# Scores of two heads through two shared buffers of two banks in a fused attention and soft-MoE kernel

## The chip, the cores and the metric

The kernel runs on one core of a Trainium2 chip. The time is device time in microseconds (us) of one execution of the whole program. A core has five engines that run their own queues of instructions: PE (matrix products; its weight loads are shown apart as PEld), DVE and ACT (element by element, with reductions on DVE), POOL (element by element too) and SP, which here only issues DMAs. On-chip memory is SBUF (128 partitions, 24 buffers of 8 KB a partition play a part here) and PSUM, where PE writes: eight banks of 128 x 512 float32.

## The reference

Attention with a local window and a few global keys, and its output, as 3072 tokens of 512, goes through a mixture of experts in which every slot is a softmax-weighted mean of all tokens:

```python
scores = scale * np.matmul(q, k.transpose(0, 1, 3, 2))            # B, H, S, D = 4, 8, 768, 64
rel = pos[:, None] - pos[None, :]
is_global = pos[None, :] < int(n_global)                          # 8 keys
is_local = (rel >= 0) & (rel < int(n_local))                      # 96 keys
scores = scores + -slopes[:, None, None] * dist                   # a slope for each head
scores = np.where(is_global | is_local, scores, -1000000000.0)
a = softmax(scores, axis=-1);  x = np.matmul(a, v)                # x: 3072 x 512
logits = x @ phi                                                  # 3072 x 32 slots
d = softmax(logits, axis=0);  c = softmax(logits, axis=1)
slot_in = d.T @ x                                                 # 8 experts x 4 slots, 512 wide
slot_out[e] = np.maximum(slot_in[e] @ w1[e], 0.0) @ w2[e]         # 512 -> 1024 -> 512
return c @ slot_out
```

(The softmaxes are abbreviated.) Everything is float32, and the products of attention weights and V are done to nearly that precision.

## The kernel before

**Units.** Attention is cut into 16 units, one for each batch b and pair of heads p. A unit's 768 queries are taken in seven blocks of keys (j); each block needs only the queries near it, so the scores of one head are seven matrices that stand side by side in 1296 columns, keys on the partitions.

**Steps of a unit u.** Each is a small function, and each issues one or a few instructions:

- `load_qk`, `load_v`: DMAs on SP's queue, into two alternating buffers for q and k and into the single buffer `vt` for V.
- `v_hi` (POOL, L490) and `v_lo` (DVE, L497): V times 64 as a float16 and the float16 of what is left of it.
- `scores(u)` (PE, L518): fourteen float32 products, seven for each head, each written as two matmuls in the profile. Head i has its own PSUM buffer `sc[i]` of three banks.
- `biased(u, i)` (DVE, L525): the eviction of head i. One custom instruction adds the table of biases and masks to 128 x 1296 scores, writes the sum to SBUF and leaves the greatest value of each partition in column i of `mx`. A small instruction behind it reads the accumulator.
- `max_t`, `max_r`, `max_b`, `max_c`: the two columns of maxima are transposed on PE (L533, into columns of `sc[1]` that the scores leave free), reduced to one number a head on DVE (L537), spread over two columns on DVE (L538), brought to all partitions on PE (L541) and copied to SBUF by ACT (L545). This maximum over a head of a unit is taken off in the exponential.
- `exponential(u, i)` (ACT, L548), `w_hi` (ACT, L551, the float16 of the weights), `w_lo` (POOL, L555, the float16 of what is left, in three parts a head; some parts are put on DVE as `w_lo_dve`).
- `values(u, i)` (PE, L575): 39 float16 matmuls, high by high, high by low and low by high, into one bank `x`. A column of ones in V gives the sums of the weights.
- `ev_sum`, `ev_rec`, `ev_mul` (DVE, L580, L584, L590): the sums, their reciprocals, and the eviction times the reciprocals into `xn`.
- `tr`, `tr_copy` (PE L603, ACT L608): x transposed in two halves, of four and three blocks; `logits` (PE L633, every second unit), and at the end of a batch the softmax pieces (`strip_...`, `by_token`) and the weighted sum of tokens (`dispatch`).

**What sets the order.** No scheduler does. The table `ORDER` (L51, 608 steps before) is a list of steps with their units, written by hand, and it is run from front to end:

```python
    for name, u, *args in ORDER:
        steps[name](u, *args)
```

So the order of the table is the order of the instructions on each engine, SP's DMAs included. The units overlap: around the maximum of unit u stand low parts and values of units u - 1 and u - 2. Engines wait for each other through semaphores where a buffer must be written or become free.

**Buffers.** Four float32 buffers `tp` hold the biased scores and later the weights of a head, and, in their last columns, the float16 high parts (two of them) and low parts (the other two). One bank holds `x`, one bank (`psm`) the transposes, logits and the rest, six the scores.

**The experts.** Their weights are 32 pieces of 1.05 MB. Twelve have buffers of their own (`wp`, `NW = 12`); twelve more places are attention's own buffers, which `free` steps load, part by part, when attention has used them for the last time. The parts of these buffers that attention doesn't use at all are loaded earlier, one at a time behind `load_v` (`extras`). Eight pieces are left. They take the places of pieces of the first layer once the first four experts' hidden layer has read them: four pieces in halves into places 0 to 3, four in quarters into places 4 and 8 to 10. Behind attention come the hidden layer (`hidden`, L106), its transposes (L120), the combining weights by slot (`weights_by_slot`, L170), the second layer (`project`, L136), its outputs (`slots_out`, L181) and the combination (`combine`, L196 to L202) with the output's DMAs.

## Time and profile before

| what | value |
|---|---|
| median of 3 runs | 238.98 us (236.74 to 241.77) |
| the profiled execution: span | 237.6 us (the page gives no other time of it) |
| PE, PEld busy | 185.2 us (78%), 142.3 us (60%) |
| DVE busy | 156.6 us (66%) |
| ACT, POOL busy | 120.4 us (51%), 118.8 us (50%) |
| DMA | 61.39 MB, 258 GB/s on the mean |
| instructions | 6476 |

A busy share is the time in which an engine ran something, as a share of the span. In the views that follow, a line such as `L525` is a line of the kernel's file, a group's row gives count, busy us, mean ns of one and the idle time just before its instructions with what ended it, and the chain of waits gives start, length, engine, buffer and line of each piece of the path that ended last. The page names a buffer without its number, so `sc` stands for both of them.

Over the whole span the profile divides into three: until about 31 us the first unit comes up, from there to about 174 us the units follow each other, some 10 us end attention and start the experts, and the last 53 us are the experts. POOL has work only until the end of attention.

### The profile page before, as it was taken

What the parts mean: (1) busy time and instruction counts of PE and PEld (TensorE: products, weight loads), DVE (VectorE), ACT (ScalarE), POOL (GpSimd) and SP (SyncE); (2) the same over time, 40 slices, a digit from 0 to 9 for tenths busy, and PEclk for the clock granted to TensorE, in tenths of its full rate; (3) what the DMA queues carried; (4) which work ended last, traced back from release to release, by engine and by line L of the source; (5) the groups of instructions that cost most, each with busy time, mean ns of one, the idle gap of its engine ahead of it and who ended that gap; (6) DMA issues with size and microseconds to landing.
All of it is one profiled execution on the core that took longest, in us unless ns stands there. A gap on an engine that the chain in (4) does not pass through costs nothing.

```text
span 237.6 us, 6476 instructions
## 1 busy us (share of the span) xinstructions
PE 185.2 (78%) x2676; PEld 142.3 (60%) x2676; DVE 156.6 (66%) x375; ACT 120.4 (51%) x167; POOL 118.8 (50%) x142
## 2 busy tenths in 40 slices
PE   8463869599698887988985987887688999999800
PEld 2453859587586776876864876766555326666600
DVE  4766192966859759669878696796757783524710
ACT  2001553758839557787764796778522155212500
POOL 7310067395959949978984888889300000000000
PEclk9965555999979999999999999997999999999975
DMA  5795784499996967257336168589799699938895
GB/s 159 274 405 196 316 321 179 125 394 349 372 390 194 415 259 242 69 203 251 103 129 217 21 229 290 151 261 304 254 302 393 206 392 400 384 111 278 293 338 169
DMA packets 20630, 61.39 MB, mean 258 GB/s; under 512 B 1904, under 2 KB 9200, under 8 KB 19056
## 3 DMA queue, kind: packets, MB, share of 16 engines
q1 hardware_dynamic: 20448, 60.89, 71.8%
q8 instruction: 23, 0.38, 0.6%
q14 instruction: 15, 0.12, 0.1%
q10 hardware_dynamic: 144, 0.00, 0.0%
HBM read 54.59 MB, written 6.29 MB: 256 GB/s over the span
## 4 chain that ended last, share of the span: by engine, by line
PE 45%; DVE 29%; issue 8%; POOL 7%; DMA 4%; ACT 2%; DVEq 0%; POOLq 0%; SPq 0%
PE sc L518 17%; DVE tp L525 13%; PE op L136 6%; PE hp L106 6%; PE x L575 6%; DVE v L497 5%; POOL tp L555 4%; DMA vt<-in_v_dram 3%; PE sc L533 2%; PE m L603 2%; DVE mr L537 2%; PE ctp L170 2%; DMA out_dram<-tp 1%; DVE rc L584 1%; DVE mm L538 1%
## 5 line engine op out<-in xcount | busy, mean ns | idle before, releaser
L555 POOL TENSOR_TENSOR tp<-tp 128x432 f16<-128x432 f32 x45 | 49.7, 1132 | 25.2 <-DVE tp L562 17.5
L555 POOL TENSOR_TENSOR tp<-tp,tp 128x432 f16<-128x432 f32 x44 | 49.0, 1140 | 12.7 <-ACT tp L551 8.4
L575 PEld LDWEIGHTS <-tp 128*128 128x128 f16 x1248 | 45.3, 102 | 13.7 <-DVE xmax L590 11.1
L575 PE MATMUL x<-v,tp 128*128 128x65 f16 (+1 forms) x1209 | 46.0, 199 | 8.9 <-DVE xmax L590 8.1
L518 PE MATMUL sc<-raw 64*128 64x216 f32 (+2 forms) x448 | 47.0, 365 | 1.6 <-DMA raw<-in_qk_dram 1.6
L518 PEld LDWEIGHTS sc<-raw 64*128 64x128 f32 x448 | 44.4, 212 | 5.2 <-DMA raw<-in_qk_dram 2.5
L548 ACT ACTIVATE tp<-tp,nb 128x1296 f32<-128x1296 f32 x32 | 44.1, 1377 | 0.6
L551 ACT CAST tp<-tp 128x1296 f16<-128x1296 f32 x30 | 38.2, 1274 | 7.0 <-PE x L575 6.2
L537 DVE TENSOR_REDUCE mr<-sc 2x1 f32<-2x128 f32 x16 | 4.5, 278 | 32.4 <-PE sc L518 32.4
L525 DVE CUSTOM_DVE_ANT_1 tp<-sc,tt 128x1296 f32<-128x1296 f32 x16 | 23.8, 1498 | 1.0 <-POOL tp L555 0.9
L603 PE MATMUL m<-ident,xn 120*128 120x120 f32 x109 | 17.8, 281 | 8.4 <-DVE xmax L590 6.1
L490 POOL TENSOR_SCALAR v<-vt 128x896 f16<-128x896 f32 x16 | 15.0, 940 | 14.5 <-DMA vt<-in_v_dram 12.2
L608 ACT COPY xta<-m 128x480 f32<-128x480 f32 (+1 forms) x21 | 10.1, 480 | 20.4 <-PE m L603 20.3
L590 DVE CUSTOM_DVE_ANT_1 xn<-x,rc 120x448 f32<-120x448 f32 x31 | 19.3, 623 | 1.0
L497 DVE SCALAR_TENSOR_TENSOR v<-vt,v 128x896 f16<-128x896 f32 x16 | 18.4, 1150 | 1.2 <-POOL v L490 1.2
L603 PEld LDWEIGHTS m<-ident,xn 120*128 120x128 f32 x109 | 11.3, 143 | 10.9 <-issue 4.9
L545 ACT COPY nb<-sc 128x2 f32<-128x2 f32 x16 | 2.6, 161 | 28.5 <-DVE mx L525 20.0
L533 PE MATMUL sc<-ident,mx 128*2 128x64 f32 x64 | 7.0, 239 | 8.6 <-DVE mx L525 8.1
L541 PE MATMUL sc<-mm,bsel 128*128 128x2 f32 x32 | 6.3, 266 | 8.2 <-DVE mm L538 7.3
L525 DVE CUSTOM_DVE_ANT_1 tp<-sc,xtt 128x1296 f32<-128x1296 f32 x8 | 12.0, 1499 | 0.5 <-POOL tp L555 0.4
L525 DVE CUSTOM_DVE_ANT_1 tp<-sc,vt 128x1296 f32<-128x1296 f32 x8 | 12.0, 1497 | 0.0
L541 PEld LDWEIGHTS sc<-mm,bsel 128*128 128x128 f32 x32 | 5.2, 203 | 11.2 <-DVE mm L538 8.4
(191 smaller groups left out, 263.6 us busy)
## 6 DMA issues: line engine op xcount, KB each, us to landing
raw<-in_qk_dram SPq DMA_DIRECT2D x15, 832.0 KB, 5.5
wp<-in_w_dram SPq DMA_DIRECT2D x12, 1024.0 KB, 9.5
vt<-in_v_dram SPq DMA_DIRECT2D x16, 448.0 KB, 4.1
wp<-in_w_dram SPq DMA_DIRECT2D x8, 512.0 KB, 8.3
wp<-in_w_dram SPq DMA_DIRECT2D x16, 256.0 KB, 5.4
out_dram<-tp SPq DMA_DIRECT2D x8, 512.0 KB, 6.7
tp<-in_w_dram SPq DMA_DIRECT2D x4, 648.0 KB, 5.5
out_dram<-vt SPq DMA_DIRECT2D x4, 512.0 KB, 4.2
```

The source lines that it names most:

```text
L106: nc.tensor.matmul(out=hp[n][32 * s:32 * s + 32, :], lhsT=slv(a, c, s), rhs=w1(e, c // 2)[:, (c % 2) * DF + 512 * n:(c % 2) * DF + 512 * n ...
L136: nc.tensor.matmul(out=o[32 * s:32 * s + 32, 0:w], lhsT=ht[:, c, 32 * s:32 * s + 32], rhs=w2(4 * a + s, half)[:, c0 + c * w:c0 + c * w + w ...
L490: nc.gpsimd.tensor_scalar(out=vhi[u % 2][:, :, :, 0:D], in0=vraw, scalar1=V_SC, scalar2=0.0, op0=ALU.mult, op1=ALU.add)
L497: nc.vector.scalar_tensor_tensor(out=vlo[k].rearrange("p j i d -> p (j i) d"), in0=vraw.rearrange("p j i d -> p (j i) d"), scalar=V_SC, in ...
L518: nc.tensor.matmul(out=sc[i][:, bk, at:at + n], lhsT=r_[r, KCOL[j]:KCOL[j] + KR], rhs=r_[r, KW + KB * j:KW + KB * j + n], start=True, stop ...
L525: nc.vector.tensor_tensor_reduce(out=tb(u, i).rearrange("p (k c) -> p k c", k=3), in0=sc[i][:, :, 0:BW], in1=table.banks(2 * (u % NP) + i) ...
L548: nc.scalar.activation(out=tb(u, i), in_=tb(u, i), func=AF.Exp, bias=nbs[u][:, i:i + 1], scale=T_SC)
L551: nc.scalar.copy(out=blocks(phi_[i])[:, :, 0:QW], in_=tb(u, i).rearrange("p (s c) -> p s c", c=QW))
L555: (engine or nc.gpsimd).tensor_tensor(out=blocks(plo_[i])[:, c, 0:QW], in0=tb(u, i).rearrange("p (s c) -> p s c", c=QW)[:, c], in1=blocks( ...
L575: nc.tensor.matmul(out=x[:, (D + 1) * t:(D + 1) * t + d], lhsT=w[:, c:c + P], rhs=vv[:, j, i, 0:d], start=(z == 0), stop=(z == len(ops) - ...
L590: nc.vector.tensor_tensor_reduce(out=xnb[(u // 2) % 3][:, :, c:c + D], in0=xps.pop((u, i))[:, :, 0:D], in1=rcs.pop((u, i)).unsqueeze(2).to ...
L603: nc.tensor.transpose(out=m[:, at:at + KB], in_=xnb[(u // 2) % 3][:, t, P * (p % 2):P * (p % 2) + P], identity=ident[0:KB, 0:KB])
```

## The change

- **Scores.** `scores(u, k)` makes a third of a unit's scores, for both heads: the blocks of bank k. The two buffers `sc[0]` and `sc[1]` have two banks each, one bank a head, and are used in turn over all thirds of all units.
- **Evictions.** `biased(u, k)` evicts a third for both heads at once, 128 x 2 x 432. The second and third take the running maximum of the one before as the start value, read from memory (`mx[:, k-1:k]`). The buffer that they write holds both heads; there are three such buffers `tb`, used in turn by units. The float16 parts are in two buffers of their own, `ph0` and `ph1`.
- **Maximum.** One maximum for both heads: one transposing matmul (L534) into a bank of `psm`, one reduction (L537) straight into the operand of the next matmul, one column broadcast. The instruction that spread two maxima (L538 of before) is gone, and so is the second matmul of each step. Both heads' exponentials use the same column.
- **Values.** `xx` has two banks, one a head. `ev_sums` and `ev_recs` take both heads in one instruction each. `psm` has two banks.
- **V.** `vt` holds two units' V, in halves, used in turn.
- **Weights.** `NW` is 9 and thirteen attention buffers become places, so 22 pieces of 32 have one before the hidden layer and ten take places over: five in halves into places 0 to 4, five in quarters into places 8 to 12. Parts unused by attention are loaded by `extra` steps of their own. `free` steps carry 11.90 MB of weights at the end of attention, where they carried 11.15.
- **Order.** The table is new, 629 steps. All six low parts of unit 0 are on POOL (three were on DVE), and in units 14 and 15 five parts are on DVE.

The core of the diff:

```diff
-NW = 12
+NW = 9
-ORDER = [('load_qk', 0), ('load_v', 0), ('load_qk0', 0), ('load_qk', 1), ('keys', 0), ('v_hi', 0), ('scores', 0),
+ORDER = [('load_qk0', 0), ('load_phis', 0), ('load_qk', 0), ('load_v', 0), ('keys', 0), ('load_qk', 1),
...
-    psm = banks.enter_context(tc.tile_pool(name="psm", bufs=1, space=PSUM))
+    psm = banks.enter_context(tc.tile_pool(name="psm", bufs=2, space=PSUM))
...
-    tps = [keep.tile([P, TW + PW // 2], F32, name=f"tp{i}") for i in range(4)]
+    tbt = [keep.tile([P, 2 * TW], F32, name=f"tb{i}") for i in range(3)]
+    pht = [keep.tile([P, WP], F32, name=f"ph{i}") for i in range(2)]
...
-    vraw = vt[:, 0:VC].rearrange(by_head, j=NJ, i=2)
+    vraw = [vt[:, VC * i:VC * i + VC].rearrange(by_head, j=NJ, i=2) for i in range(2)]
...
     def load_v(u):
-        nc.sync.dma_start(out=vraw, in_=v[u // NP, u % NP])
-        if u > 2 and extras:
+        nc.sync.dma_start(out=vraw[u % 2], in_=v[u // NP, u % NP])
+
+    def extra(i):
+        if extras:
             k, c0, c1 = extras.pop(0)
             load_w([k], c0, c1)
...
-    sc = [pss.tile([P, 3, 512], F32, name=f"sc{i}", tag=f"sc{i}") for i in range(2)]
+    sc = [pss.tile([P, 2, 512], F32, name=f"sc{k}", tag=f"sc{k}") for k in range(2)]
+    xx = psx.tile([P, 2, 512], F32, name="x", tag="x")
...
-    def scores(u):
+    def scores(u, k):
         r_ = rq[u % 2]
-        for j in range(NJ):
-            bk = next(k for k in range(3) if j in BANK_J[k])
-            n, at = QN[j], COL[j] - BW * bk
+        z = sc[(3 * u + k) % 2]
+        at = 0
+        for j in BANK_J[k]:
+            n = QN[j]
             for i in range(2):
                 r = slice(D * i, D * i + D)
-                nc.tensor.matmul(out=sc[i][:, bk, at:at + n], lhsT=r_[r, KCOL[j]:KCOL[j] + KR],
+                nc.tensor.matmul(out=z[:, i, at:at + n], lhsT=r_[r, KCOL[j]:KCOL[j] + KR],
                                  rhs=r_[r, KW + KB * j:KW + KB * j + n], start=True, stop=True)
+            at += n
...
         nc.vector.tensor_tensor_reduce(
-            out=tb(u, i).rearrange("p (k c) -> p k c", k=3), in0=sc[i][:, :, 0:BW], in1=table.banks(2 * (u % NP) + i),
-            scale=1.0, scalar=-3.0e38, op0=ALU.add, op1=ALU.max, accum_out=mxs[u][:, i:i + 1])
+            out=tb(u)[:, :, BW * k:BW * k + BW], in0=sc[(3 * u + k) % 2][:, :, 0:BW], in1=table.unit(u % NP, k),
+            scale=1.0, scalar=-3.0e38 if k == 0 else mx[:, k - 1:k], op0=ALU.add, op1=ALU.max, accum_out=mx[:, k:k + 1])
...
     def max_t(u):
-        mx = mxs.pop(u)
-        for z in range(2):
-            nc.tensor.matmul(out=sc[1][0:2, 1 + z, BW:BW + 64], lhsT=mx, rhs=ident[:, 64 * z:64 * z + 64], start=True, stop=True)
+        ms[u, "m"] = m = bank(("max", u))
+        nc.tensor.matmul(out=m[0:1, 0:P], lhsT=mxs.pop(u)[:, 2:3], rhs=ident, start=True, stop=True)
     def max_r(u):
-        mr = wk.tile([2, 1], F32, name="mr", tag="mr", bufs=2)
-        nc.vector.tensor_reduce(out=mr, in_=sc[1][0:2, 1:3, BW:BW + 64], axis=AX.XY, op=ALU.max)
-        nc.vector.tensor_scalar(out=mms[u % 2][0:2], in0=ident[0:2, 0:2], scalar1=mr, scalar2=None, op0=ALU.mult)
+        nc.vector.tensor_reduce(out=mms[u % 2][0:1], in_=ms[u, "m"][0:1, 0:P], axis=AX.X, op=ALU.max)
...
-        x = bank(("values", u, i))
+        x = xx[:, i]
...
+    def ev_sums(u):
+        nc.vector.tensor_tensor(out=rsall[:, 2 * u:2 * u + 2, :], in0=xv[:, :, :, D], in1=eps.unsqueeze(1).to_broadcast([KB, 2, NJ]), op=ALU.add)
+
+    def ev_recs(u):
+        rc = wk.tile([KB, 2, NJ], F32, name="rc", tag="rc", bufs=3)
+        for i in range(2):
+            rcs[u, i] = rc[:, i]
+        nc.vector.reciprocal(out=rc, in_=rsall[:, 2 * u:2 * u + 2, :])
...
             for c in (0, WP // 2):
-                load_w(range(npl, 28), c, c + WP // 2)
+                load_w(range(npl, npl + 5), c, c + WP // 2)
         else:
             for c in range(0, WP, WP // 4):
-                load_w(range(28, 32), c, c + WP // 4)
+                load_w(range(npl + 5, 32), c, c + WP // 4)
```

How this stands on the engines. First DVE in the middle of attention, one unit's period, before: a maximum, the low part of V, then one head's eviction, the normalisation of an earlier unit's head, the other head's eviction. (The numbers behind a name are the program's own; `ISA` is the custom instruction, and the row behind it its accumulator's read.)

```order
L537 TENSOR_REDUCE mr<-sc_177 2x1
L538 TENSOR_SCALAR mm_162<-ident,mr 2x2
L497 SCALAR_TENSOR_TENSOR v_101<-vt,v_101 128x896
L525 ISA tp_99,mx<-sc_176,tt 128x1296
L525 ISA mx 128x1
L580 TENSOR_TENSOR rsall<-x,eps 120x7
L584 RECIPROCAL rc<-rsall 120x7
L590 ISA xn_106,xmax<-x,rc 120x7x64
L590 ISA xmax 120x1
L525 ISA tp_100,mx<-sc_177,tt 128x1296
L525 ISA mx 128x1
```

And DVE at the same place now:

```order
L527 ISA tb_94,mx<-sc_171,tt 128x2x432
L527 ISA mx 128x1
L527 ISA tb_94,mx<-sc_172,tt,mx 128x2x432
L527 ISA mx 128x1
L527 ISA tb_94,mx<-sc_171,tt,mx 128x2x432
L527 ISA mx 128x1
L500 SCALAR_TENSOR_TENSOR v_99<-vt,v_99 128x896
L537 TENSOR_REDUCE mm_160<-m 1x1
L588 TENSOR_TENSOR rsall<-x,eps 120x14
L594 RECIPROCAL rc<-rsall 120x14
L600 ISA xn_104,xmax<-x,rc 120x7x64
L600 ISA xmax 120x1
```

The three evictions now follow each other, the low part of V stands between the last of them and the reduction instead of behind it, and both heads are normalised together behind that.

PE around the maximum, before: half a transposed unit, the maxima's transposes, and then at once the scores of the next unit, head by head in turn.

```order
L603 MATMUL m<-ident,xn_106 128x120 x3
L533 MATMUL sc_177<-ident,mx 2x64 x2
L518 MATMUL sc_176<-raw_96 128x216
L518 MATMUL sc_177<-raw_96 128x216
L518 MATMUL sc_176<-raw_96 128x216
L518 MATMUL sc_177<-raw_96 128x216
```

PE around a maximum now:

```order
L518 MATMUL sc_171<-raw_92 128x216 x2
L518 MATMUL sc_171<-raw_92 128x168 x2
L518 MATMUL sc_171<-raw_92 128x48 x2
L612 MATMUL m<-ident,xn_105 128x120 x7
L518 MATMUL sc_172<-raw_93 128x216 x4
L534 MATMUL m<-ident,mx 1x128
```

The last third of this unit's scores, a whole transposed unit, and the first third of the next unit's scores (its q and k are in `raw_93`) stand ahead of the maximum's matmul, which has a bank of its own.

Last, SP's queue at the loads that take over places in the hidden layer, before:

```order
L371 DMA wp_83<-in_w_dram 128x1024
L371 DMA wp_84<-in_w_dram 128x1024
L371 DMA wp_85<-in_w_dram 128x1024
L371 DMA wp_86<-in_w_dram 128x1024
L371 DMA wp_83<-in_w_dram 128x1024
```

And now:

```order
L372 DMA wp_83<-in_w_dram 128x1024
L372 DMA wp_84<-in_w_dram 128x1024
L372 DMA wp_85<-in_w_dram 128x1024
L372 DMA wp_86<-in_w_dram 128x1024
L372 DMA wp_87<-in_w_dram 128x1024
L372 DMA wp_83<-in_w_dram 128x1024
```

A fifth first half stands ahead of the second halves; behind the five second halves follow quarters of five pieces where there were four.

More of the change, by code (lines that the diff above doesn't have):

```diff
@@ L480, in tile_attention_moe @@
         n = 0
+        pool = None
         def tile(self, shape, dtype, name, tag):
+            if self.pool is None:
+                scp.close()
+                self.pool = banks.enter_context(tc.tile_pool(name="psl", bufs=1, space=PSUM))
             self.n += 1
-            return free_banks[0].tile(shape, dtype, name=name, tag=f"l{(self.n - 1) % 6}")
-    free_banks = []
-    LAST_BANKS = (("values", last, 1), ("tr", last, 1), ("logits", last))
+            k = self.n % 6
+            if k < 4:
+                return self.pool.tile(shape, dtype, name=name, tag=f"l{k}")
+            return psm.tile(shape, dtype, name=name, tag="m")
@@ L876, in tile_attention_moe @@
     obs = [places[16 + i // 2][:, 4 * HF * (i % 2):4 * HF * (i % 2) + 4 * HF] for i in range(6)]
[L877 removed]
+    ops = [xx[:, n] for n in range(2)]
     def project(n, a, cs=range(8)):
```

109 lines of the change are left out of this document (51 added, 58 removed).

## The prediction, made before the changed kernel ran

> **What bounds the kernel now.** I first read the busy shares, then the windows of busy time by stage, then the chain that ended last, and last the groups by line with the waits. The windows (length, then the busy time of PE, PEld, DVE, ACT and POOL, the granted clock, DMA share, GB/s):
>
> ```profile
> 76.55:150.45 73.90, 61.42 (x1081) 52.29 (x1082) 57.58 (x137) 52.09 (x69) 60.09 (x57) 1.00 0.58 204
> 110.00:120.00 10.00, 9.20 (x162) 7.13 (x160) 9.28 (x25) 8.44 (x14) 8.71 (x9) 1.00 0.57 197
> 192.00:208.00 16.00, 16.00 (x177) 8.87 (x173) 8.75 (x25) 6.97 (x13) 0.00 (x0) 1.00 1.03 390
> 210.00:212.00 2.00, 2.00 (x46) 1.21 (x42) 0.68 (x2) 0.00 (x0) 0.00 (x0) 1.00 0.10 33
> ```
>
> The first row spans eight units, from the maximum of unit 6 to that of unit 14: 73.90 / 8 = 9.24 us a unit. Per unit PE is busy 7.68, POOL 7.51, DVE 7.20, ACT 6.51. No engine is full, so a loop of waits sets the 9.24. The chain shows that loop (start, length, what):
>
> ```profile
> 7.23 0.92 POOL v L490
> 8.17 1.09 DVE v L497
> ...
> 10.39 0.21 DVE tt L261 x2
> 10.62 0.40 DVE tt L270
> 11.16 1.51 DVE tp L525
> ...
> 14.84 4.78 PE sc L518 x28
> ...
> 52.80 6.23 DMA vt<-in_v_dram
> ...
> 76.55 0.39 PE sc L533 x4
> 76.94 2.49 PE sc L518 x28
> 79.45 0.29 DVE mr L537
> ...
> 80.76 1.00 DVE v L497
> 81.75 1.42 DVE tp L525
> ...
> 84.16 1.42 DVE tp L525
> 85.64 0.39 PE sc L533 x4
> ...
> 168.12 1.13 DVE tp L555 x2
> ...
> 170.99 0.60 PE m L603 x4
> ...
> 172.77 0.34 PE m L603 x3
> 173.11 1.20 PE l L575 x39
> ...
> 176.80 0.93 PE l L633 x4
> ...
> 184.53 13.87 PE hp L106 x128
> ...
> ...
> 215.12 5.79 PE op L136 x104
> ```
>
> From 76.55 to 85.64 the chain goes through all the scores of a unit (2.49), the reduction, the low part of V, two evictions with the normalisation between them, and the next maximum. The next scores can't start before the second eviction, because both heads' buffers are read until then; so PE waits for DVE and DVE for PE:
>
> ```profile
> DVE mr L537 <- PE sc L518: 32.4, 15, 4.0
> POOL v L490 <- DMA vt<-in_v_dram: 12.2, 6, 4.8
> SPq L391 <- DVE v L497: 50.0, 14, 13.1
> ```
>
> DVE sits 32.4 us before the reductions alone. The load of V (SP's queue, third row) waits for the only buffer, and the load itself is on the chain at 52.80.
>
> **The change, part by part.** Durations (count, then busy us and mean ns of one, then idle time before):
>
> ```profile
> L525 DVE CUSTOM_DVE_ANT_1 tp<-sc,tt 128x1296 f32<-128x1296 f32 x16 | 23.8, 1498 | 1.0 <-POOL tp L555 0.9
> L590 DVE CUSTOM_DVE_ANT_1 xn<-x,rc 120x448 f32<-120x448 f32 x31 | 19.3, 623 | 1.0
> L538 DVE TENSOR_SCALAR mm<-ident,mr x16: 216/664/1055, 20.0 to 161.1; 2x2 f32<-2x2 f32 x16
> L548 ACT ACTIVATE tp<-tp,nb 128x1296 f32<-128x1296 f32 x32 | 44.1, 1377 | 0.6
> L551 ACT CAST tp<-tp 128x1296 f16<-128x1296 f32 x30 | 38.2, 1274 | 7.0 <-PE x L575 6.2
> L580 DVE TENSOR_TENSOR rsall<-x,eps 120x7 f32<-120x7 f32 x31 | 4.9, 158 | 3.7 <-PE x L575 3.4
> L584 DVE RECIPROCAL rc<-rsall 120x7 f32<-120x7 f32 x32 | 6.4, 199 | 1.0
> L555 POOL TENSOR_TENSOR tp<-tp 128x432 f16<-128x432 f32 x45 | 49.7, 1132 | 25.2 <-DVE tp L562 17.5 <-ACT tp L551 7.7
> 31.42 3.23 POOL L555 TENSOR_TENSOR tp<-tp 128x432 f16<-128x432 f32 x3 [17.52 <-DVE tp L562]
> ```
>
> *Evictions.* Three of 864 elements replace two of 1296. The same custom instruction has two sizes here, so (1498 - 623) / (1296 - 448) = 1.03 ns an element and 161 ns fixed: 1.05 us each, 3.16 against 3.00 a unit, +0.16, and one more accumulator read, about +0.08. The second and third take their start value from memory, which no eviction does now. The bounds of that are 0 and the median wait of L538, 0.66; L538's row shows 0.22 at the least. I take 0, as L590, an eviction with one operand from SBUF and one from PSUM like these, keeps to 623 beside a working POOL; the 0.66 goes to the rivals. *Maximum.* L538 goes (-0.66 on DVE, its median), two of four first matmuls go (about -0.2 of L533's 0.39). *Normalisation.* One sum and one reciprocal for two heads: -0.16 - 0.20. DVE's unit becomes 7.20 + 0.24 - 0.66 - 0.36 = 6.42. But the low part of V (L497) now meets the running POOL instruction that L538 waited for, up to 0.66 - 0.22 = 0.44, so 6.42 to 6.86; DVE stays below PE. PE's unit is 7.68 less 0.2, POOL's 7.51 as before.
>
> *Order and buffers.* The next unit's first scores stand ahead of this unit's maximum, so the loop above is cut: PE has other work while DVE evicts. A unit then costs at least 7.5 us (PE full) and at most the 9.24 of now. Between them I take the fullest stretch that this program reached, the second window row: PE 9.20 of 10, thus 7.68 / 0.92 = 8.35. I don't go lower, since POOL (7.51), DVE and PE would all have to be over nine tenths full in one fixed order.
>
> *Start.* The low part of V (8.17, 1.09) moves behind the first evictions, and the 1.1 before it, waiting for POOL's high part, goes too: first eviction at 11.16 - 2.2 = 8.96. Three evictions (3.2), one table (0.6, as the two rows ahead of 11.16), the maximum (0.39 as at 85.64, 0.29 as at 79.45, and some 0.3 for its broadcast and copy), one exponential (L548: 1.38) and one high part (L551: 1.27) give the first low part on POOL at 16.4, where the last row above has 31.42. All six low parts of unit 0 now lie on POOL: 6.0 and 0.9 of waiting. So unit 1 starts at 23.3 and unit 2 at 30. To that I add 2 for PE at half clock (the scores take 4.78 instead of 2.49 at 14.84). Bounds 0 and four units of (4.78 - 2.49) = 9; 2 because PE is the fuller here.
> By the Trainium skill (TensorE: Matmul & The Clock Gate, Part 1) some 3.4 us of sustained matmuls lift the clock, and by that the 2 would be 0; the trace disagrees, as 4.78 us of scores at 14.84 ran at half clock to their end.
>
> *V doubled.* The 6.23 of DMA on the chain goes; what comes late next there is POOL's low part, which the 8.35 holds.
>
> *Weights.* Nine whole buffers instead of twelve; 22 places instead of 24, so ten pieces of 1.05 MB load late instead of eight: 2.1 MB / 390 GB/s = 5.4 us more DMA. The late loads end now at about 210.3 (the last window row: 0.10 of its 2 us), and the last 64 of the 104 matmuls at 215.12 need the last piece, at 215.12 + 40/104 x 5.79 = 217.3. So 7.0 us of cover hide 5.4, cost 0. If the cover is gone, 5.4. Also SP now waits for a fifth place before the second halves; the first four halves, 2.1 MB, keep DMA busy 5.4 us meanwhile. The frees at the end of attention carry 11.9 MB instead of 11.15: +1.9 us of DMA, before loads that are needed 10 us later; 0.
>
> *End of attention.* Three half transposes and the logits of unit 13 now stand behind the last values. On PE that is about 2.5 (two second halves of a transpose, 0.34 each, a first half, 0.60, the logits, 0.93, and some 0.3 for a copy that they wait for), beside 1.6 of DVE work for unit 15 (0.16 + 0.20 + 2 x 0.62): +0.9.
>
> **The sum**, against the profiled execution's span of 237.6 (the page gives no other time of it; the median of the runs is 238.98, 1.4 above). Now the values end at 173.11 + 1.20 = 174.3. After: 30 + 2 + 13 x 8.35 for unit 15's low parts at 140.6, then 6.2 for that unit as now (168.12 to 174.3, three of its low parts on DVE) = 146.8. That is -27.5; with +0.9, 237.6 - 26.6 = 211.0, and 1.4 above it 212.4. I say 213.
>
> **Rivals.**
> A, the sum above.
> B, the wait only moves: the unit stays at 9.24, since the low part of V now stands ahead of the reduction on DVE (its 1.07 plus a wait for POOL), and PE's queue stops at the maximum's second matmul. For it: four engines at 6.5 to 7.7 of 9.24. Against: PE has scores behind the first matmul. 13 x 0.89 = +11.6: 225.
> C, PE stays at half clock through units 0 to 3. For it: the page's row of 40 slices (5.94 us each, tenths of full clock), 0.5 to 0.6 from slice 3 to slice 7, thus until about 41, and short bursts of scores between evictions now.
>
> ```profile
> PEclk9965555999979999999999999997999999999975
> ```
>
> Against: the loop that spaced them is cut. +9 - 2: 220.
>
> D, the start value from memory makes each second and third eviction hold the SBUF port that POOL also needs. For it: rows of two-operand or pointer instructions that waited:
>
> ```profile
> L684 DVE SCALAR_TENSOR_TENSOR state<-state,al x3: 211/964/964, 117.6 to 180.2; 128x1 f32<-128x1 f32 x3
> ```
>
> The same instruction took 0.21 with POOL idle (the first of the three numbers) and 0.96 beside it. Against: L590's 623. POOL's unit would be 7.51 + 2 x 1.05 = 9.6, and 10.9 if the two waits of 0.66 come on top: 213 + 13 x (9.6 to 10.9 - 8.35) = 229 to 246. It is slower than before from 10.7 us a unit on; its upper end, 244 to 246, is the case on the other side.
> The Trainium skill (SBUF — State Buffer, "SBUF: two separate sides") gives that port to a Vector instruction with two SBUF inputs or in a two-port mode, for its whole length, and does not name a scalar; by that D doesn't happen, and no run here shows it yet.
> E, the late loads miss their cover because attention's end frees its buffers faster than DMA fills them: +5.4: 218.
>
> **Chances.** A 0.52, B 0.20, C 0.08, E 0.06; D 0.14, of which 0.06 within 2% and 0.08 slower. Within 2% of 238.98 (234.2 to 243.8, about what a measurement of this kernel can tell from no change) stands nothing else. So faster 0.86, same 0.06, slower 0.08. A's own range is 205 (7.7 a unit) to 221; the range for 8 in 10 takes in B, C and E: 205 to 229.
>
> **What would show it.** Right: the unit's period, from maximum to maximum, at 8.0 to 8.7 with PE over 0.9 busy; the first low part on POOL near 16; the reduction no longer waiting for scores; the hidden layer's matmuls starting near 158 and 53 before the end. B shows as a period over 9 with PE waiting for DVE's reduction; C as clock 0.5 beyond 30 us; D as later evictions well over 1.2 us and stretched low parts; E as the projection waiting for a load. The prediction is wrong if the first evictions start after 11 us, or if a fifth wait that I haven't named takes PE's share below 0.85.

## The result and the profile after

The changed kernel takes 219.34 us (median of 4 runs, 217.11 to 220.11) where the kernel before takes 237.86 on the same chip (4 runs, 236.58 to 241.77): a ratio of 0.919 with a 95% interval of 0.910 to 0.928. The prediction said 213 in a range of 205 to 229. The profiled execution has a span of 217.8 us, where the prediction's sum had 211.0. All ratios leave out executions in a slower state that some of the timed ones fell into, so a ratio isn't always the quotient of two medians.

First the windows of busy time after the change (length, then busy time of PE, PEld, DVE, ACT and POOL, granted clock, DMA share, GB/s), for the eight units from the maximum of unit 6 to that of unit 14, and for the experts:

```profile
64.23:128.82 64.59, 62.13 (x1021) 49.60 (x1018) 55.34 (x127) 51.03 (x69) 59.13 (x56) 1.00 0.58 196
162.78:217.80 55.02, 40.40 (x479) 22.97 (x479) 24.18 (x52) 15.32 (x27) 0.00 (x0) 0.92 0.87 311
```

A unit takes 64.59 / 8 = 8.07 us instead of 9.24, and PE is busy for 0.96 of it (62.13 / 64.59), POOL for 0.92. The second row is the part that attention doesn't touch; it is 1.9 us longer than before (53.1).

The chain that ended last (start, length, what), at the places that answer to those shown of before:

```profile
8.50 0.99 DVE tt L261 x2
9.51 0.40 DVE tt L269
10.04 1.06 DVE tb L527
11.16 1.97 PE sc L518 x12
13.16 1.12 DVE tb L527
...
15.02 1.74 PE sc L518 x8
16.76 0.52 PE m L540 x2
...
20.25 2.56 POOL ph L558 x3
...
149.99 1.35 PE x L575 x39
...
162.78 13.87 PE hp L106 x128
...
190.46 0.15 DVE flag L858
190.61 1.49 PE x L136 x24
```

Three things are to be seen. Twelve score matmuls still take 1.97 us at 11.16, and eight take 1.74 at 15.02: PE runs at half clock there. The values of unit 15 end at 149.99 + 1.35 = 151.3, where they ended at 174.3. And in the tail 24 matmuls of the projection wait for an instruction of DVE at 190.46, which nothing did before. Between the pieces shown, the chain goes mostly through POOL's low parts (L558, 20% of the span) from 20 to about 82 us, and mostly through PE's matmuls from there to the end of attention, so PE alone doesn't set all units.

The low parts of the weights on POOL (start, length, and in brackets the idle time before and what ended it), for units 0 to 2, and the last group of unit 15:

```profile
20.25 7.03 POOL L558 TENSOR_TENSOR ph<-tb,ph 128x432 f16<-128x432 f32 x6 [8.15 <-ACT ph L551]
31.59 6.20 POOL L558 TENSOR_TENSOR ph<-tb,ph 128x432 f16<-128x432 f32 x6 [4.31 <-ACT ph L551]
39.52 6.69 POOL L558 TENSOR_TENSOR ph<-tb,ph 128x432 f16<-128x432 f32 x6 [0.82 <-ACT ph L551]
...
145.20 3.72 POOL L558 TENSOR_TENSOR ph<-tb,ph 128x432 f16<-128x432 f32 x3 [2.10 <-ACT ph L551]
```

With these the prediction's sum can be laid beside the trace, term by term:

| term | predicted | measured | difference |
|---|---|---|---|
| start of unit 2's low parts | 32 | 39.5 | +7.5 |
| 13 units to unit 15's low parts | 13 x 8.35 = 108.6 | 145.2 - 39.5 = 105.7 | -2.9 |
| from there to the end of the values | 6.2 | 6.1 | -0.1 |
| to the hidden layer's first matmul | 10.2 + 0.9 = 11.1 | 162.8 - 151.3 = 11.4 | +0.3 |
| from there to the end | 53.1 | 55.0 | +1.9 |
| span (rounded parts) | 211.0 | 217.8 | +6.8 |

So the start is what the sum had most wrong, the middle was a little better than forecast, and the tail has a wait that wasn't named. The experiments take these in turn.

The groups of the instructions in dispute (count, then busy us, mean ns of one, then idle time before):

```profile
L558 POOL TENSOR_TENSOR ph<-tb,ph 128x432 f16<-128x432 f32 x91 | 101.4, 1147 | 21.5 <-ACT ph L551 21.1
L500 DVE SCALAR_TENSOR_TENSOR v<-vt,v 128x896 f16<-128x896 f32 x16 | 23.2, 1452 | 0.0
L527 DVE CUSTOM_DVE_ANT_1 tb<-sc,tt,mx 128x864 f32<-128x864 f32 x16 | 17.9, 1117 | 5.4 <-PE sc L518 4.8
L527 DVE CUSTOM_DVE_ANT_1 tb<-sc,tt 128x864 f32<-128x864 f32 x8 | 8.5, 1058 | 5.2 <-PE sc L518 4.8
```

An eviction takes 1.06 us, as worked out (1.05); with a start value from memory 1.12. The low part of V rose from 1.15 to 1.45 us in the mean, by 0.30, within the 0.44 that the prediction gave as the bound.

### The profile page after: what moved, and what is told of

Its sections match the earlier page's. It is cut to its first block, busy times and chain, and to the rows that moved or that the text cites. A ratio compares the mean times of both kernels' runs of the same rounds, so it can differ in the third digit from the quotient of the medians.

```text
span 217.8 us, 6430 instructions
## 1 busy us (share of the span) xinstructions
PE 183.6 (84%) x2644; PEld 135.3 (62%) x2644; DVE 151.6 (70%) x355; ACT 121.4 (56%) x169; POOL 121.5 (56%) x141
## 4 chain that ended last, share of the span: by engine, by line
PE 41%; POOL 22%; DVE 15%; issue 10%; DMA 3%; ACT 3%; POOLq 0%; DVEq 0%; ACTq 0%; SPq 0%
POOL ph L558 20%; PE x L575 9%; PE x L136 7%; PE hp L106 6%; PE sc L518 6%; DVE ph L558 3%; DVE xn L600 2%; PE m L642 2%; PE m L612 2%; POOL v L493 2%; ACT ph L551 2%; DMA nraw<-in_n_dram 2%; DMA out_dram<-v 2%; DVE v L500 2%; PE ctp L170 2%
## 5 line engine op out<-in xcount | busy, mean ns | idle before, releaser
L558 POOL TENSOR_TENSOR ph<-tb,ph 128x432 f16<-128x432 f32 x91 | 101.4, 1147 | 21.5 <-ACT ph L551 21.1
L551 ACT CAST ph<-tb 128x1296 f16<-128x1296 f32 x32 | 40.6, 1270 | 16.3 <-PE x L575 15.6
L575 PE MATMUL x<-v,ph 128*128 128x65 f16 (+1 forms) x1248 | 44.0, 195 | 6.5 <-DVE xmax L600 5.3
L575 PEld LDWEIGHTS <-ph 128*128 128x128 f16 x1248 | 41.1, 98 | 12.5 <-issue 5.7
L548 ACT ACTIVATE tb<-tb,nb 128x1296 f32<-128x1296 f32 x32 | 43.5, 1375 | 0.3
L527 DVE CUSTOM_DVE_ANT_1 tb<-sc,tt,mx 128x864 f32<-128x864 f32 x16 | 17.9, 1117 | 5.4 <-PE sc L518 4.8
L527 DVE CUSTOM_DVE_ANT_1 tb<-sc,tt 128x864 f32<-128x864 f32 x8 | 8.5, 1058 | 5.2 <-PE sc L518 4.8
L527 DVE CUSTOM_DVE_ANT_1 tb<-sc,xta,mx 128x864 f32<-128x864 f32 x8 | 8.9, 1118 | 2.4 <-PE sc L518 2.0
L106 PE MATMUL hp<-wp,sl 128*32 128x512 f32 x72 | 10.5, 594 | 0.0
L527 DVE CUSTOM_DVE_ANT_1 tb<-sc,xtt,mx 128x864 f32<-128x864 f32 x8 | 8.9, 1116 | 1.2 <-POOL v L493 0.6
L534 PE MATMUL m<-ident,mx 128*1 128x128 f32 x32 | 6.5, 286 | 2.5 <-DVE mx L527 2.5
```

Of the source, the lines that this page charges most:

```text
L106: nc.tensor.matmul(out=hp[n][32 * s:32 * s + 32, :], lhsT=slv(a, c, s), rhs=w1(e, c // 2)[:, (c % 2) * DF + 512 * n:(c % 2) * DF + 512 * n ...
L527: nc.vector.tensor_tensor_reduce(out=tb(u)[:, :, BW * k:BW * k + BW], in0=sc[(3 * u + k) % 2][:, :, 0:BW], in1=table.unit(u % NP, k), scal ...
L548: nc.scalar.activation(out=t, in_=t, func=AF.Exp, bias=nbs[u], scale=T_SC)
L551: nc.scalar.copy(out=blocks(phi_[i])[:, :, 0:QW], in_=tb(u)[:, i].rearrange("p (s c) -> p s c", c=QW))
L558: (engine or nc.gpsimd).tensor_tensor(out=blocks(plo_[i])[:, c, 0:QW], in0=tb(u)[:, i].rearrange("p (s c) -> p s c", c=QW)[:, c], in1=bloc ...
L575: nc.tensor.matmul(out=x[:, (D + 1) * t:(D + 1) * t + d], lhsT=w[:, c:c + P], rhs=vv[:, j, i, 0:d], start=(z == 0), stop=(z == len(ops) - ...
```

## The experiments

Each kernel below is the changed one with the edit shown, unless said otherwise. The medians are of 4 runs each; the ratios are to the kernel before on the same chip. Not all experiments ran on one chip, and the kernel before has medians of 237.9 to 240.6 us on them, so a difference of two experiments' times is only good to about 2 us.

### The start: PE's clock

The granted clock in half microseconds of the changed kernel (length, busy time of PE, count, granted clock, DMA share, GB/s):

```profile
7.50:8.00 0.50, 0.13 (x2) 1.00 1.01 426
...
11.00:11.50 0.50, 0.34 (x2) 0.59 1.13 475
...
31.00:31.50 0.50, 0.50 (x6) 0.50 0.00 0
31.50:32.00 0.50, 0.50 (x12) 0.93 0.07 16
```

PE's last matmul before its first long gap ended at 7.63; DVE's first eviction, which must free a buffer, came at 10.04. At about 11.1, 3.5 us after that matmul, the clock is halved, and it comes back at about 31.6. The first experiment fills the gaps with small matmuls into a bank that nothing uses yet (a step that the program already has, three matmuls each):

```diff
 ('scores', 0, 1),
+('warm_x', 0), ('warm_x', 0), ('warm_x', 0), ('warm_x', 0), ('warm_x', 0), ('warm_x', 0),
...
 ('scores', 0, 2),
+('warm_x', 0), ('warm_x', 0), ('warm_x', 0),
...
 ('scores', 1, 0),
+('warm_x', 0), ('warm_x', 0), ('warm_x', 0),
...
 ('scores', 1, 2),
+('warm_x', 0), ('warm_x', 0),
```

> Fourteen groups of three small bfloat16 matmuls fill PE's gaps between the first scores (six groups behind the second third of unit 0, three, three and two further on); nothing else changes. Theory 1 (the start is late because PE falls to half clock at 11.1 us, 3.5 us after its last matmul, and stays there to 31.5): the granted clock stays at 1.0, eight score matmuls take 1.0 us instead of 1.81 and twelve 1.0 instead of 1.95, the first low part on POOL comes at 18.5 to 19.5 instead of 20.25, unit 1's at 26 to 28 instead of 31.6, and the whole is 3 to 5 us faster, about 215. Rival (the start is held by the chain of evictions, exponentials and low parts, whatever the clock): unit 1's first low part stays within 1 us of 31.6 and the time within 1 us of 219.

Measured: 215.02 us, ratio 0.903 (0.891 to 0.915), and a span of 214.6. The clock by slices of a fortieth of the span, from the page of the changed kernel and then of this one:

```profile
PEclk9955569999999999999999999999999999999965
```

```profile
PEclk9999999999699999999999999999999999999955
```

And its low parts on POOL:

```profile
18.28 7.05 POOL L558 TENSOR_TENSOR ph<-tb,ph 128x432 f16<-128x432 f32 x6 [6.34 <-ACT ph L551]
25.54 6.20 POOL L558 TENSOR_TENSOR ph<-tb,ph 128x432 f16<-128x432 f32 x6 [0.21 <-ACT ph L551]
32.61 2.94 POOL L558 TENSOR_TENSOR ph<-tb,ph 128x432 f16<-128x432 f32 x3
```

Theory 1 holds: unit 1 starts 6.05 us earlier, unit 2 39.52 - 32.61 = 6.9. The half clock thus costs 6.9 us by unit 2, where the prediction's sum had 2 for it: 4.9 of the 7.5 us by which the start was late. The other 2.6 stay with the gaps filled, as unit 2 then starts at 32.6 and not at 30. The chain shows how the half clock costs so much: with two buffers the third third of scores waits for the first eviction, the broadcast of the maximum stands behind a third of the next scores, and the first values stand behind more scores, so most matmuls at half clock lie on the path. Only 217.8 - 214.6 = 3.2 us of it reach the end of the profiled executions (the medians differ by 4.3); the rest is given back in units 3 to 6, which the section on a faster version takes up. The two ratios' intervals overlap (0.891 to 0.915 and 0.910 to 0.928), so the claim rests on the traces.

The Trainium skill (TensorE: Matmul & The Clock Gate, Part 1) says that the clock is halved after an idle window of some 3.4 us and given back after as long a busy one. The trace agrees with the first at this place (3.5 us here; the last section has a fall after a shorter gap) and not with the second: PE worked without a gap from 23.35 to 31.6, 8.2 us, before the clock returned.

Does the change bring this cost, or do both kernels bear it? The kernel before, with its gaps filled in the same way:

```diff
 ('scores', 0),
+('warm_x', 0), ('warm_x', 0), ('warm_x', 0), ('warm_x', 0), ('warm_x', 0), ('warm_x', 0), ('warm_x', 0), ('warm_x', 0),
...
 ('max_b', 0),
+('warm_x', 0), ('warm_x', 0), ('warm_x', 0), ('warm_x', 0), ('warm_x', 0), ('warm_x', 0),
```

> The kernel before the change, with PE's gaps at the start filled in the same way (eight groups of small matmuls behind the first scores, six behind the first broadcast). It tells whether the half clock is a cost that the change brought or one that both kernels bear. Theory (both bear it: before, PE falls to half clock at 13.4 us and stays there to 40.6, and its 28 score matmuls then take 4.8 us instead of 2.5): full clock from the start, three units each about 2 us earlier, whole 4 to 6 us faster than before, 233 to 235. Rival (before, the start is held by DVE's low parts of unit 0 and by tables): within 1.5 us of before.

Measured: 234.39 us, ratio 0.984 (0.972 to 0.995). Both bear it: with both kernels' gaps filled the change's ratio is 0.903 / 0.984 = 0.918, and with neither's it is 0.919. The filling isn't complete here: the granted clock is still halved from 27.0 to 33.8 us and from 85.0 to 91.9. Rival C of the prediction (half clock through units 0 to 3) thus happened in the changed kernel, by the prediction's own sign of a clock of 0.5 beyond 30 us, though it ended after unit 2's scores. Its price of 7 us more than the forecast was about what the start lost in all; the forecast's own 2 us for it should have been nearer the upper bound of 9.

### The middle: the loop that was cut

All scores of the next unit, and the eviction that stood between them, go back behind this unit's maximum, for units 2 to 14:

```diff
-('scores', 4, 0),
...
-('biased', 4, 0),
...
 ('max_t', 3),
...
-('scores', 4, 1),
...
-('scores', 4, 2),
...
 ('max_b', 3),
+('scores', 4, 0), ('biased', 4, 0), ('scores', 4, 1), ('scores', 4, 2),
```

> For units 2 to 14 all scores of the next unit (and the evictions of it that stood earlier) are put behind this unit's last maximum matmul, as before the change; buffers and instructions stay as changed. Theory 1 (the gain of the middle came from cutting the loop of scores, eviction and maximum): PE waits for DVE's last eviction, the low part of V and the reduction, some 2 us a unit of which half is filled by values and transposes, so the period goes from 8.0 to 9.0 to 10 us and the whole to 232 to 245. Rival (the gain came from fewer instructions and the second V buffer): the period stays below 8.3 and the whole below 223.

Measured: 230.62 us, ratio 0.969 (0.957 to 0.982); the period of units 6 to 14 is 71.95 / 8 = 8.99. The period is at the lower edge of what theory 1 said (9.0), the time 1.4 us below its range. PE around one maximum (start, length, what, idle before in brackets), first in the changed kernel:

```profile
113.46 0.38 PE L534 MATMUL m<-ident,mx 128*1 128x128 f32 x2
113.77 0.53 PE L612 MATMUL m<-ident,xn 120*128 120x120 f32 x3
114.22 1.00 PE L518 MATMUL sc<-raw 64*128 64x216 f32 x8
115.16 0.38 PE L540 MATMUL m<-mm,bsel 2*128 2x1 f32 x2
```

and here:

```profile
119.93 0.38 PE L534 MATMUL m<-ident,mx 128*1 128x128 f32 x2
120.24 0.53 PE L612 MATMUL m<-ident,xn 120*128 120x120 f32 x3
121.52 0.38 PE L540 MATMUL m<-mm,bsel 2*128 2x1 f32 x2 [0.75 <-DVE mm L537]
121.82 1.73 PE L518 MATMUL sc<-raw 64*128 64x216 f32 x16
```

A third of the scores between the transpose and the broadcast covers DVE's reduction; without it PE stands 0.75 us here and 6.5 us in all (10 times), and scores wait for an eviction 7.5 us (8 times) instead of 4.7 (2 times). Taking back the order alone loses 230.62 - 219.34 = 11.3 us of the 18.5 that the change gained. A part of that is the clock again: in this kernel it was halved from 106.3 to 109.7 us and from 143.8 to 147.2. No run has the old score buffers with the rest of the change, so what the two shared buffers are worth by themselves isn't shown, only what the order is worth that they allow.

The next kernel tests the prediction's rival B, that the low part of V ahead of the reduction on DVE sets the unit. For the V of units 2 to 14:

```diff
-('v_lo', 6),
 ('max_t', 7),
...
 ('max_r', 7),
+('v_lo', 6),
```

(The low part of unit 10's V is made from unit 12's V in this kernel; the instructions are the same.)

> On DVE the reduction of the maximum stands ahead of the low part of V in every unit, as before the change; all else as changed. Theory 1 (the unit of 8.0 us is set by PE, 0.96 busy): 0 to -2 us, 217 to 219. Rival (the low part of V, 1.45 us in the mean, lies in the loop that sets the unit): the period falls to 7.2 to 7.6 and the whole to 207 to 213.

Measured: 230.75 us, ratio 0.970 (0.957 to 0.983). Neither theory had that. Who waited for whom, in total, times and longest, in the changed kernel:

```profile
PE x L575 <- DVE xmax L600: 5.3, 7, 1.3
...
DVE mm L537 <- PE m L534: 1.2, 2, 0.8
```

and here:

```profile
PE x L575 <- DVE xmax L600: 14.6, 14, 1.9
...
DVE mm L537 <- PE m L534: 12.0, 14, 1.2
```

The transposed maximum isn't there yet when DVE has evicted: PE has half a transposed unit or a third of scores ahead of it. The low part of V fills that wait. Put behind the reduction it fills nothing, DVE stands 0.9 us a unit, and the normalisation behind both comes later, which holds the bank that the next values need. Rival B had the sign of this instruction's place wrong.

Rival D was that a start value from memory holds the port that POOL needs. With a constant start and one more reduction:

```diff
-            scale=1.0, scalar=-3.0e38 if k == 0 else mx[:, k - 1:k], op0=ALU.add, op1=ALU.max, accum_out=mx[:, k:k + 1])
+            scale=1.0, scalar=-3.0e38, op0=ALU.add, op1=ALU.max, accum_out=mx[:, k:k + 1])
...
-        nc.tensor.matmul(out=m[0:1, 0:P], lhsT=mxs.pop(u)[:, 2:3], rhs=ident, start=True, stop=True)
+        mx = mxs.pop(u)
+        nc.vector.tensor_reduce(out=mx[:, 3:4], in_=mx[:, 0:3], axis=AX.X, op=ALU.max)
+        nc.tensor.matmul(out=m[0:1, 0:P], lhsT=mx[:, 3:4], rhs=ident, start=True, stop=True)
```

> Each eviction starts from a constant and leaves its maximum in a column of its own; one more small reduction on DVE takes the greatest of the three ahead of the transpose. All else as changed. Theory (the start value from memory costs its 0.06 us an eviction and no port): evictions 1.06 instead of 1.12, the added reduction takes about as much back, period 8.0 to 8.2, whole 218 to 221. Rival D of the prediction (the pointer holds the port that POOL needs): POOL's low parts go from 1.147 us towards 1.0 and the whole is 3 us faster or more.

Measured: 232.46 us, ratio 0.969 (0.960 to 0.977). The edit had put the small reduction into the step of the transpose, and so, on DVE, behind the low part of V; the transpose then waited for both (PE for 11.6 us in all, 12 times). It was repeated with the reduction directly behind the third eviction:

```diff
...
+        if k == 2:
+            nc.vector.tensor_reduce(out=mx[:, 3:4], in_=mx[:, 0:3], axis=AX.X, op=ALU.max)
```

> Constant start value again, with the reduction of the three maxima directly behind the third eviction, ahead of the low part of V. Theory (the 13 us of the run before came from the transpose waiting behind the low part of V, and the pointer itself costs 0.06 us an eviction): DVE's unit as with the pointer, -0.12 + 0.15; whole 218 to 221. Rival D (the pointer holds POOL's port): 3 us or more faster than 219.3. Second rival (something else in the constant form costs): stays near 232.

Measured: 218.68 us, ratio 0.919 (0.909 to 0.929), the same as the changed kernel's. Its groups:

```profile
L560 POOL TENSOR_TENSOR ph<-tb,ph 128x432 f16<-128x432 f32 x91 | 101.3, 1146 | 19.0 <-ACT ph L553 18.5 <-PE sc L518 0.5
...
L527 DVE CUSTOM_DVE_ANT_1 tb<-sc,tt 128x864 f32<-128x864 f32 x24 | 24.7, 1056 | 9.8 <-PE sc L518 9.4
...
L531 DVE TENSOR_REDUCE mx<-mx 128x1 f32<-128x3 f32 x16 | 2.5, 156 | 0.6
```

POOL's low parts take 1146 ns with constants and 1147 with pointers, so D doesn't happen; the pointer costs 0.06 us an eviction, 0.12 a unit, which the extra reduction of 0.156 gives back. By the Trainium skill (SBUF — State Buffer, "SBUF: two separate sides") a Vector instruction with at most one SBUF input, outside the two-port modes, doesn't contend with POOL; these two numbers agree, if a start value doesn't count as an input; the Trainium skill doesn't say whether it does. The pair of runs shows something else as well: between two positions on DVE of an instruction of 0.156 us lie 13.8 us by the times and 12 by the ratios (0.969 and 0.919 on two chips), since the way from the third eviction to the transpose is on the loop of every unit.

### V's second buffer

V goes back into one half, each load behind the low part of the unit before:

```diff
-    vraw = [vt[:, VC * i:VC * i + VC].rearrange(by_head, j=NJ, i=2) for i in range(2)]
+    vraw = [vt[:, 0:VC].rearrange(by_head, j=NJ, i=2) for i in range(2)]
...
-('load_v', 8),
...
 ('v_lo', 7),
+('load_v', 8),
```

> V in one half of its buffer for all units, each load of V behind the low part of the unit before (its place when there was one buffer); all else as changed. Theory 1 (the second buffer only hides the load's 4.7 us where weights are loading too, up to about 66 us): POOL's high part waits for the load in four or five early units, 1 to 2 us each, and the period later stays 8.0; whole +2 to +7, about 223. Rival (the second buffer is needed in every unit): the period is 9 or more throughout and the whole is over 230. Third (it buys nothing): within 1 us of 219.

Measured: 234.26 us, ratio 0.987 (0.974 to 1.000). Weights that take V's place at the end were written over unit 15's V ahead of its low part, which then waited for them. With these loads exchanged (the free half first):

```diff
-('free', 9),
+('free', 10),
...
-('free', 10),
+('free', 9),
```

> V in one half of its buffer for all units as in the run before, and the weights that take V's place at the end now load into the free half first, so that the last V isn't waited for behind weights. Theory 1, as the run before left it (its maxima of unit 15 came 5.3 us later than with two buffers, and another 8 us were the misplaced load of weights): whole +5 to +6, 224 to 226. Rival (the end costs the 8 us anyway): 232 to 234.

Measured: 233.77 us, ratio 0.979 (0.968 to 0.990). Theory 1 of this run falls, its rival holds. Of the first run's rival only the time came (over 230): the period of units 6 to 14 is 8.5 here and there, not 9. The wait of POOL for V, in the changed kernel and then here:

```profile
POOL v L493 <- DMA vt<-in_v_dram: 1.7, 1, 1.7
```

```profile
POOL v L493 <- DMA vt<-in_v_dram: 30.2, 8, 10.3
```

The reduction of unit 15 comes at 145.2 instead of 137.6, so 7.6 us are lost in the units before (5.3 in the profiled execution of the first run, where it comes at 142.9). The rest is the last V: its load can be issued only at 145.3, when the low part of unit 14's V is made. It stands behind three loads of weights into buffers that attention has left, and lands at 153.0 with the DMA engines full; POOL stands 10.3 us for it. So the second buffer is worth about 14 us in this order. This and the 11.3 of the order don't add up: each is what is lost when only that part is taken back.

### The tail and the late weights

One buffer of weights fewer, so eleven pieces load late instead of ten:

```diff
-NW = 9
+NW = 8
...
-('piece', 8),
```

> Eight buffers for weights instead of nine, so eleven pieces load late instead of ten. Theory (the late loads of the changed kernel end at 192.9 us, 3.9 us ahead of the matmuls at 196.8 that need the last of them): 1.05 MB more is 2.7 us of DMA, which the 3.9 still hides; 0 to +1 us, about 219.5. Rival E of the prediction (the cover is gone already): +2 to +3, about 222, and the last 64 matmuls of the projection wait for a load.

Measured: 218.31 us, ratio 0.905 (0.899 to 0.912): no loss. Rival E doesn't happen; there is cover for 2.7 us of loads more.

The new wait of the tail, by giving the second half of the projection a bank of its own:

```diff
-            k = self.n % 6
+            k = self.n % self.banks
...
-    ops = [xx[:, n] for n in range(2)]
+    left.banks = 4
+    ops = [xx[:, 0], psm.tile([P, 512], F32, name="op", tag="m")]
```

> The second half of the projection gets a bank of its own instead of the second bank of the values' buffer; the other temporary results of the experts' part use four banks instead of six from there. Theory (24 matmuls wait 1.1 us for DVE's reading of the first bank because both banks are one buffer to the dependencies): they follow the matmul ahead of them at once, the part from the hidden layer's start to the end falls from 55.0 to 53.9 us or somewhat less far if four banks are few; whole about 218.3. Rival (the wait is for something else on DVE): 55.0 and 219.3 stay.

Measured: 219.35 us, ratio 0.910 (0.903 to 0.917), a span of 217.7. Its chain at that place:

```profile
189.49 1.35 PE op L136 x22
190.84 3.29 PE cp L196 x20
194.13 5.79 PE op L136 x104
```

The matmuls follow at once, so the wait came from both banks being one buffer to the dependencies, as the theory said. But 20 matmuls of the combination take 3.29 us on four banks instead of 2.59, and the part from the hidden layer on is 217.7 - 162.8 = 54.9 us instead of 55.0. Of the wait's 1.1 us nothing reached the end in this form; six banks with the wait gone weren't tried. From the hidden layer to the last 104 matmuls it is 30.6 us before the change, 31.9 in the changed kernel and 31.3 here; behind these matmuls it is 16.7, 17.3 and 17.8. So what the wait adds to the 1.9 us isn't shown, and what the rest is stays open: the output's DMAs, which run to the end of the program in both kernels, weren't tried by themselves.

### A faster version

With the start at full clock, the five periods from unit 2's reduction to unit 7's take 9.4, 7.2, 8.5, 9.3 and 8.9 us in the kernel with filled gaps, and the DMA engines are nearly full there. Seven pieces of weights are put later:

```diff
 ('load_qk', 6),
+('piece', 2),
...
 ('load_qk', 12),
+('piece', 8),
```

> The kernel with PE's gaps filled at the start, and seven of the nine whole pieces of weights loaded two to five units later, each behind the load of q and k of units 6 to 12. Theory (with the start 6.9 us earlier, the loads of q, k and weights of units 2 to 6 collide: q and k land 6.6 us after their issue in the median instead of 4.9, and units 3 to 7 take 9.4, 7.2, 8.5, 9.3 and 8.9 us): these periods fall to 7.3 to 8.3 and the whole to 209 to 213. Rival (PE's order or its dip to half clock at 54 to 59 us sets them): the periods stay and the time is within 1 us of 215.

Measured: 213.40 us, ratio 0.886 (0.880 to 0.892), a span of 213.1; the interval lies below that of the changed kernel, so this version beats it and the kernel before (that of the kernel with filled gaps alone it just touches). The expectation held in the sum only: one period fell (9.3 to 7.7), the others stayed at 9.4, 7.1, 8.5 and 9.0, so these loads weren't what held them. The period that fell is also the one in which the clock had dipped (last section); which of the two it was isn't separated.

Last, the start's order: the reduction and the broadcast of units 0 to 2 directly behind the transpose, and the first V behind q and k of unit 1.

```diff
 ('max_t', 0),
+('max_r', 0), ('max_b', 0),
 ('scores', 1, 1),
-('max_r', 0),
...
-('max_b', 0),
```

> The kernel with filled gaps and later weights, and in units 0 to 2 the reduction and the broadcast of the maximum directly behind its transpose, ahead of scores and of the low part of V; the first load of V stands behind q and k of unit 1. Theory (at the start each unit's exponentials wait for the broadcast, which stands behind a third of scores, and the first bias table waits for POOL's high part of V): first eviction at 9.2 to 9.5 us instead of 10.04, first low part on POOL 1.0 to 1.5 us earlier than 18.3, unit 2's 1 to 2 us earlier than 32.6, whole 211 to 212.5. Rival (what is won at the start is given back by unit 3, whose period of 9.4 us is set by something that doesn't move): 213.4 +- 0.5.

Measured: 214.51 us, ratio 0.902 (0.891 to 0.912): no gain. At the start it did as said (first eviction at 8.78 us, first low part on POOL at 16.64, where the prediction had 8.96 and 16.4), but unit 2's low parts came at 32.55, as without it (32.66): the rival holds for the first three units. The profiled span was 211.4, 1.7 less than the version above; the timed runs don't show that, so it isn't claimed.

## Why the prediction was right, and where it was not

- **The bound and the loop: right.** No engine was full, a loop of scores, evictions and maximum set 9.24 us a unit, and cutting it brought PE to 0.96 busy. Putting the scores back behind the maximum costs 11.3 us. Of the prediction's signs the period (8.07), PE's share and the reduction came; the first low part on POOL (20.25, not 16) and the hidden layer's start (162.8, not 158) were late.
- **The unit's period: right in mechanism, 0.2 to 0.3 us too long.** PE's share was taken as 0.92, from the fullest stretch before; it is 0.96, with a busy time of 62.13 / 8 = 7.77 a unit instead of 7.68. The 0.2 us that two matmuls fewer were to save on PE don't show. DVE's unit is 6.92, just above the 6.42 to 6.86 of the prediction, POOL's 7.39 instead of 7.51.
- **The start: wrong by 7.5 us, and the main step is the clock's term.** "2 because PE is the fuller here" took a value near the lower bound of 0 to 9; it measured 6.9 by unit 2. PE was the fuller only later: its first gap is 3.5 us long, since with two buffers the third third of scores waits for the first eviction. The other 2.6 us are in the chain ahead of the low parts: the first eviction came at 10.04 instead of 8.96, because the high part of V still ran beside DVE's table work (two small copies 0.99 us instead of 0.21), and the maximum's broadcast stood behind a third of scores (1.74). With both moved and the gaps filled, in the last experiment, the first low part came at 16.64, where the prediction had 16.4.
- **How near the sum came is in part luck.** The middle's 2.9 us in hand come with the late start: from unit 2's reduction to unit 15's it is 103.6 us in the changed kernel and 107.0 with the gaps filled. So one error of the sum gave back a part of another; that is why 219.3 lies 6 us from 213 and not some 9.
- **V doubled: right in sign, too small in size.** It was priced as the 6.23 us of one load on the chain; taken back in this order, it is 233.77 - 219.34 = 14.4, about half of it for the last unit's V alone. The two aren't the same question, since the load is taken back here in an order made for two buffers.
- **Late weights: right.** The 5.4 us are hidden, and 2.7 more would be.
- **The tail: a wait that wasn't named.** 1.1 us, from two banks that the dependencies see as one buffer; that the end would come earlier without it isn't shown. The prediction had read that the outputs of the projection moved to `xx`, and hadn't asked what else is tied to it.
- **Rivals.** B, D and E didn't happen. C did, beside the forecast's own case: its 220 is nearer to 219.3 than the 213 is, but not by its own sum alone, as only 3.2 to 4.3 us of the half clock reached the end, the middle was 2.9 us shorter and the tail 1.9 longer.

## What to carry to other kernels

A gap of PE is priced twice, by its length and by the clock behind it: where a row shows half clock, price every matmul on the path until the clock is back, not a share of them. In a fixed order, ask of each instruction which wait it fills and what stands between a result and its reader: the same 0.156 us on DVE cost nothing ahead of one instruction and 12 to 14 us behind it. When two buffers become one for the sake of a wider instruction, look at everything else that uses either half.

## What wasn't expected of the hardware

The clock can fall after much shorter gaps than at the start. In the kernel with filled gaps PE ran nothing from 52.9 to 54.0 only (the same columns as in the half microseconds above):

```profile
52.50:53.00 0.50, 0.35 (x2) 1.00 1.03 419
53.00:53.50 0.50, 0.00 (x0) 1.00 1.21 391
53.50:54.00 0.50, 0.00 (x0) 1.00 0.79 303
54.00:54.50 0.50, 0.46 (x12) 0.80 1.13 367
54.50:55.00 0.50, 0.50 (x14) 0.50 0.85 293
...
57.00:57.50 0.50, 0.50 (x4) 0.50 0.89 363
57.50:58.00 0.50, 0.50 (x5) 0.79 1.14 451
```

After 1.2 us without a matmul the clock is halved at 54.3, and after 3.4 us it is back, where at the start 3.5 us of idleness went ahead of the fall and 8.2 us of work ahead of the return.

Read in steps of 0.2 us, the twelve traces that have such stretches between their first matmuls and the output show 24 of them, and each lasts a whole multiple of 3.41 us: 3.41 here, 20.48 (six times) in the changed kernel, 27.31 (eight times) in the kernel before. PE was busy for at most 0.64 of the 3.41 us ahead of a fall, and for 0.86 or more of those ahead of a return. That isn't all that decides: in the changed kernel PE worked without a gap from 14.50 to 17.92, and in the second kernel with a constant start value from 14.36 to 17.77, on scores and the maximum's matmuls both times, and the clock came back only in the second. What decides it stays open.
